# An adaLN block with sliding dilated attention and an MLP: softmax denominators from a ones column of V, K and Q weights loaded by halves, V of the first batch in four pieces, and another written-out order

## The chip, the cores and the metric

The kernel runs on one core of a Trainium2 chip. The core has a matrix engine (TensorE, PE in the profile, with its weight loads as PEld), a vector engine (VectorE, DVE), an activation engine (ScalarE, ACT), a general engine (GpSimd, POOL) and a queue engine (SyncE, SP), which here issues nearly all DMAs. The metric is the device time of one execution in microseconds (us); lower is better. All engines work through their own instructions in order and wait for each other by semaphores.

## The reference

S = 2048 rows, D = 448, H = 16 heads of 28, window of 8 keys at distance 2, F = 1792; all inputs are bf16.

```python
mod = silu(c) @ w_mod                      # six vectors of 448: sa, ca, ga, sb, cb, gb
h = layernorm(x) * (1 + ca) + sa
q, k, v = split_heads(h @ wqkv)
# key w of row s is row s - 2*w, for w = 0..7; rows before 0 are masked
attn = softmax(q . k / sqrt(28))           # over the 8 keys
x = x + ga * (attn @ v) @ wo
h = layernorm(x) * (1 + cb) + sb
x = x + gb * (gelu(layernorm(h) @ w1 + b1) @ w2 + b2)
```

## The kernel before

**Layout.** Even and odd rows never meet in the attention, so the sequence is two interleaved streams of 1024 rows (NS = 2), which lie side by side in every tile. The rows are cut into 8 tiles p of 128 (times 2 streams). D = 448 is three blocks of 128 and a rest of 64 rows; the rest's matmuls are those at L553, in 64-row tiles of the array. Heads stand 32 apart (HP) in the transposed tensors, 28 of them used.

**Front (tiles in units [0], [1], [2,3], [4,5], [6,7]).** Per tile: bn_stats and bn_aggr on DVE, the power -1/2 (`rstd`, on ACT or POOL), normalize on DVE into a buffer `zy` (five of them), a copied tail, a transpose. Units 0 and 1 are transposed by TensorE; the others by a DMA transpose on SP (`zT`). Then `affine` (L501/L503) applies the modulation and gives `hT`. K and Q of units 0 and 1 come from weights spread to a 32-wide head pitch (`spread`, `Wqk`, `Wqr`); those of tiles 2 to 7 are made in natural layout from the unspread staging tiles (`natural_qk`), evacuated into a `zy` buffer and transposed by DMA into `kT`, `qT` (L630).

**Attention in 9 batches of 114 queries.** `v{i}` makes V of the batch; `lt` the logits (two halves), ACT the exponentials (L744), DVE the mask (L750). `pd{i}` (L759) multiplies the weights `et` by a matrix of ones, which gives every one of the 32 output partitions of a head the denominator; `po{i}` (L770) multiplies them by V. ACT turns the denominators into reciprocals by Ln (L779, read from PSUM) and Exp (L781); DVE multiplies (`omul`, L787) into `qT`, over the queries. The V buffer's four spare columns of each head are zero. `out_proj` then makes wo, the residual, the second and third normalization and the transposed MLP input `yT`.

**MLP in 4 tiles of 256 rows (two p each):** `w1`, Gelu on ACT, `w2`, residual, store.

**Phases.** Batches 0 to 4, then MLP tile 0; batches 5 and 6, then MLP tile 1; batches 7 and 8, then MLP tiles 2 and 3. Each switch between Exp and Gelu loads an activation table (L924, L931).

**Order.** Nothing is scheduled at run time. Each `add(...)` makes a numbered task; `ORDER` lists the numbers, and this is the order in which they are issued, so each engine's own order is the list's order restricted to that engine. A suffix (`:A`, `:D`, `:P`, `:R`) takes another engine, or for `:R` another variant. `55+12@55` issues twelve filler matmuls of 256 columns on zeros (L381) ahead of task 55. `SLOTS` gives each tile its buffer; all PSUM tiles share four double banks (room "P").

Of the kernel before, what the change touches and what calls it, by code (L numbers as in the profile page):

```python
# [9 lines left out]
FP32 = mybir.dt.float32  # L10
# [5 lines left out]
KT, KS = 4, 64  # L16
# [50 lines left out]
455 369 434 371 490 372 456 403 443 491 488 435 444 404:D 457 405 458 459 493 492 436 494 460 437 495 461 594 517 438  # L67
462 496 497 463 536 498 499 595 525 500 537 596:D 524 538 539 466 464 501 502 467 465 518 503 528 468 526 527 470 505
529 504 506 531 469 519 507 530 521 471 520 510 472 523 540 522 543 475 508 553 532 541 476 473 533 474 509 542 511
535 562 565 534 477 551 557 512 513 552 563 514 478 515:D 566 479 564 600 480 597 567 554 544 598 481 601 568 445 569  # L70
570 602 547 555 571 599 556 548 572 516 603 604 605 545 606 573 628 607 546 574 608 635 609 549 610 550 636 611 439
575 630 640 576 612 629 637 577 639 613 578 614 638 579 641 581 633 580 634 582 632 583 631 586 647 584 585 587 616
588 615 648 617 642 656 645 618 644 621 649 589 658 622 619 646 620 643 623 650 664 625 590 624 591 651 626:D 592 654
662 653 627 665 655 657 652 663 659 674 660 666 667 669 661 675 668 676 678 677 679 686 672 673 670 687 681 671 690
680 691 688 689 694 693 701 683 692 682 684 695 685 702 697 703 704 709 698 696 710 699 705 711 700 706 712 707 708
# [77 lines left out]
def kernel(  # L153
# [74 lines left out]
    ones_k = cst.tile([128, 2, HP], BF16, name="ones_k")  # L228
# [16 lines left out]
    def dconst(us, fn, writes):  # L245
        early.append(add("DVE", us, fn, writes=writes, after=[one], name="const " + writes[0]))
# [44 lines left out]
    def consts():  # L291
        for vb in vbufs:
            nc.vector.memset(vb[:, :, :, DH:HP], 0.0)
        nc.vector.memset(ones_k[:], 1.0)
        nc.vector.memset(ones_k[0:WIN - 1, 1, :], 0.0)

    dconst(0.45, consts, ["vpad", "ones"])
# [25 lines left out]
    def load_qk(kt):  # L323
        load(lambda: nc.sync.dma_start(out=wqk_st.t[:, kt, :], in_=A_wqkv[kt * 128:kt * 128 + 128, 0:2 * D + HP - DH]), 0.62, [f"wqk{kt}"],
             bufs=[wqk_st])

    def load_rest(a):
        load(lambda a=a: nc.sync.dma_start(out=wqr_st.t[KS * a:KS * a + KS, :], in_=A_wqkv[(KT - 1) * 128:D, 0:2 * D + HP - DH]),
             0.5, [f"wr{a}"], bufs=[wqr_st])
# [20 lines left out]
    for kt in range(KT - 1):  # L350
        load_qk(kt)
    load_x(1, 2)
    load_rest(0)
    load_rest(1)
    load_x(2, 4)
    load_wv()
# [33 lines left out]
    add("PE", 0.45, c_cols, mode="32x128", reads=["c", "c1", "one1", "warm_w"], bufs=[psc], fills=[psc], name="c_cols")  # L390
    add("ACT", 0.12, lambda: nc.scalar.activation(out=e_c[:], in_=psc.t[:, 0, 0:128 * KT:128], func=ACT.Exp, scale=-1.0), bufs=[psc],
# [39 lines left out]
    def spread(half):  # L431
# [3 lines left out]
        for ks in [[k] for k in range(KT - 1)]:  # L435
            k0, n = ks[0], len(ks)
            dst, src = (lambda k0=k0, n=n: Wqk[:, k0:k0 + n, half]), (lambda k0=k0, n=n: heads(wqk_st.t[:, k0:k0 + n, half * D:half * D + D], H))
            add("DVE", 0.06 + 0.18 * n, lambda dst=dst, src=src: nc.vector.tensor_copy(out=dst(), in_=src()), reads=[f"wqk{k}" for k in ks],
                bufs=[wqk_st], writes=[f"W{half}{k}" for k in ks], port=True, name="spread",
                alt={"ACT": (0.13 + 0.43 * n, lambda dst=dst, src=src: nc.scalar.copy(out=dst(), in_=src())),  # L440
                     "POOL": (0.1 + 0.5 * n, lambda dst=dst, src=src: nc.gpsimd.tensor_copy(out=dst(), in_=src()))})

        for a in range(2):
            rows, c0 = slice(KS * a, KS * a + KS), half * D + a * D // 2
            src = lambda rows=rows, c0=c0: heads(wqr_st.t[rows, c0:c0 + D // 2], H // 2)
            add("DVE", 0.22, lambda rows=rows, src=src: nc.vector.tensor_copy(out=Wqr[rows, half], in_=src()), reads=[f"wr{a}"],
# [62 lines left out]
    def front_ln(u, on_act, dma=False):  # L509
# [5 lines left out]
        for q, p in enumerate(u):  # L515
# [3 lines left out]
            rstd(0, 2 * p, 2, on_act)  # L519
# [59 lines left out]
    def front_qk(u):  # L579
        last_qk.clear()  # L580
        n, c0 = 128 * len(u), LEAD + 128 * u[0]
        for half in range(2):
# [13 lines left out]
            for k in range(2):  # L596
                first = u[0] == k == 0
                last_qk.extend(summed([item(k, a) for a in range(2)], NS * n / 2400 + 0.0025,
                                      ([] if first else [f"W{half}{k}" for k in range(KT - 1)] + [f"h{kt}_{p}" for kt in range(KT - 1) for p in u] + rk), [pqs[k]], [pqs[k]], after=last_qk[-2:] if small and k else (),
# [13 lines left out]
    def natural_qk(p):  # L613
        c0 = LEAD + 128 * p
        for half in (1, 0):
# [6 lines left out]
            summed([item(s) for s in range(NS)], 0.1895, [f"wqk{k}" for k in range(KT - 1)] + ["wr0", "wr1"] + [f"h{kt}_{p}" for kt in range(KT)],  # L622
# [54 lines left out]
    def attention(i, tbl, prev_w1):  # L677
# [19 lines left out]
        else:  # L697
            def vmm(kts, first):

                for s in range(NS):  # L700
                    for kt in kts:
                        rest = kt == KT - 1
                        rows = slice(KS * s, KS * s + KS) if rest else slice(0, 128)
                        for j in range(2):
                            nc.tensor.matmul(pv.t[WK * j:WK * j + WK, s, 0:D], lhsT=hT[rows, NS * kt + s, kc + j * WQ:kc + j * WQ + WK],  # L705
                                             rhs=Wv[rows, kt, :], start=first and kt == kts[0], stop=not first and kt == kts[-1],
# [6 lines left out]
            def v_first():  # L713
# [3 lines left out]
            add("PE", 7 * 0.1895 + 0.1, None, reads=["pads", "wv", "wvr0", "wvr1"] + [f"h{kt}_{p}" for kt in range(KT) for p in ps_], bufs=[pv, vb],  # L717
                fills=[pv], instr=32, name=f"v{i}",
                alt={"PE": (7 * 0.1895 + 0.1, v_last, "128x64", "64x64"), "PE2": (7 * 0.1895 + 0.1, v_first, "64x64", "128x64")})
# [4 lines left out]
                                                            in_=pv.t[:, :, 0:D].rearrange("p s (h d) -> p s h d", h=H)))})  # L724
        et = sb("et", [128, 4, 4 * NS, WE], BF16, "et")
# [27 lines left out]
        pd, po = psum("pd"), psum("po")  # L753

        def dmm():
            for j in range(2):
                rows = slice(WK * j, WK * j + WK)
                for r in range(4):
                    nc.tensor.matmul(pd.t[HP * r:HP * r + HP, j, 0:2 * SBE], lhsT=ones_k[rows, int(i == j == 0), :],  # L759
                                     rhs=et.t[rows, r].rearrange("p m c -> p (m c)"),  # L760
                                     start=True, stop=True, tile_position=(WK * j, HP * r))
# [200 lines left out]
```

## Time and profile before

| | |
|---|---|
| three runs | 171.62, 169.03 and 171.14 us; median 171.14 |
| profiled execution | 170.37 us, of which 168.6 us are the span from first to last instruction |
| PE busy | 160.9 us, 95% of the span |
| DVE, ACT, POOL busy | 113.2, 101.3 and 42.0 us |

In the profile, a group of instructions has its source line, engine, operation, tiles, shapes and count; then its busy time in us and the mean of one in ns; then the idle time of its engine ahead of it and who ended it. A timeline row has its start, its length, engine and line, and in brackets the engine's idle time before it with the releaser. In the rows of windows stand the busy us of each engine (and instructions) in a stretch.

### The profile page before, as it was taken

Reading aid. Unit: us, or ns where it says so; the run is one execution under the profiler, and the core shown is the slowest. Engines: PE = TensorE matmul, PEld = TensorE weight load, DVE = VectorE, ACT = ScalarE, POOL = GpSimd, SP = SyncE. Lnnn points to the kernel's source line nnn. Section 1 sums busy time; section 2 is a strip of 40 time slices with the busy share of each in tenths; the row PEclk is TensorE's granted clock in tenths of the full one; section 3 lists DMA queues with packets and bytes.
Section 4 is the critical chain, followed back from the end, with each engine's and each line's share of the span. In section 5 each row is a group of like instructions: output and inputs, shape, how many; then the busy total and the mean of one; then the engine's idle time right before and its main releaser. Section 6 shows DMA issues by size and latency. Waiting matters only on the chain.

```text
span 168.6 us, 4965 instructions
## 1 busy us (share of the span) xinstructions
PE 160.9 (95%) x2126; PEld 84.0 (50%) x2126; DVE 113.2 (67%) x277; ACT 101.3 (60%) x139; POOL 42.0 (25%) x69
## 2 busy tenths in 40 slices
PE   7999969987999999999999999999999999999992
PEld 4778535444554544435565443555544455344562
DVE  7869898758899969897837869465596940400112
ACT  3378888949379946869557167986318440099000
POOL 3235251002030400319300033850003156008100
PEclk9999999999999999999999999999999999999999
DMA  5999989699999799300150000028020006110002
GB/s 158 323 336 291 167 253 172 129 158 255 188 227 287 211 160 201 100 0 0 25 106 2 4 0 2 4 49 188 4 95 14 0 4 120 46 67 0 0 27 82
DMA packets 35573, 18.78 MB, mean 111 GB/s; under 512 B 28507, under 2 KB 34592, under 8 KB 35552
## 3 DMA queue, kind: packets, MB, share of 16 engines
q1 hardware_dynamic: 35548, 18.47, 47.6%
q8 instruction: 16, 0.26, 0.6%
q14 instruction: 5, 0.04, 0.1%
q10 hardware_dynamic: 4, 0.00, 0.0%
HBM read 9.81 MB, written 1.84 MB: 69 GB/s over the span
## 4 chain that ended last, share of the span: by engine, by line
PE 77%; DMA 13%; DVE 4%; issue 2%; POOL 2%; SPq 1%; ACT 1%; POOLq 0%; DVEq 0%
PE p L882 26%; PE p L547 22%; PE pw L802 7%; DMA zT<-zy 7%; PE pq L547 5%; PE p L553 4%; DMA x_all<-in_A_x_dram 4%; PE pv L547 3%; PE po L770 3%; DMA wm_st<-in_w_mod_dram 3%; PE lt L737 2%; DVE hT L501 2%; PE pv L705 2%; PE pd L759 1%; DVE stt L455 1%
## 5 line engine op out<-in xcount | busy, mean ns | idle before, releaser
L863 ACT ACTIVATE hm<-p,b_col 128x512 bf16<-128x512 f32 x56 | 33.6, 695 | 30.6 <-PE p L553 26.1
L882 PE MATMUL p<-w_s,hm 128*128 128x448 bf16 (+1 forms) x238 | 44.5, 342 | 0.0
L547 PE MATMUL p<-yT,w_s 128*128 128x512 bf16 x168 | 38.1, 380 | 0.0
L468 POOL TENSOR_TENSOR rs_all<-mvs,neg_half 128x2 f32<-128x2 f32 x23 | 16.4, 719 | 75.1 <-DVE mvs L457 75.1
L882 PEld LDWEIGHTS <-hm 128*128 128x128 bf16 x238 | 22.6, 98 | 18.9 <-issue 0.6
L547 PEld LDWEIGHTS <-w_s 128*128 128x128 bf16 x168 | 15.8, 98 | 21.0 <-issue 3.2
L888 DVE TENSOR_TENSOR x_all<-p,x1p 128x896 bf16<-128x896 f32 (+2 forms) x10 | 8.8, 899 | 23.7 <-PE p L882 23.7
L744 ACT ACTIVATE et<-lt 128x928 bf16<-128x928 f32 x18 | 16.1, 940 | 6.7 <-PE lt L737 6.6
L455 DVE BATCH_NORM_STATS2 stt<-x_all 128x6 f32<-128x448 bf16 x32 | 18.6, 610 | 1.6 <-DMA x_all<-in_A_x_dram 1.4
L547 PE MATMUL pq<-wqk_st,hT 128*128 128x448 bf16 x72 | 15.0, 353 | 1.8 <-DVE hT L501 1.5
L840 POOL TENSOR_TENSOR x1p<-x_all,gbb_bc 128x448 f32<-128x448 bf16 x16 | 16.5, 1060 | 0.0
L787 DVE TENSOR_TENSOR qT<-po,den 128x912 bf16<-128x912 f32 x9 | 10.0, 1106 | 7.1 <-ACT den L781 6.7
L802 PE MATMUL pw<-wo_s,qT 128*128 128x448 bf16 x64 | 13.1, 353 | 0.0
L750 DVE TENSOR_TENSOR et<-et,mask 128x928 bf16<-128x928 bf16 x18 | 11.0, 640 | 2.2 <-ACT et L744 2.1
L627 ACT CAST zy<-pq 128x896 bf16<-128x896 f32 x11 | 9.7, 911 | 2.7 <-issue 2.0
L809 DVE TENSOR_TENSOR x_all<-pw,x_all 128x896 bf16<-128x896 f32 x8 | 8.7, 1088 | 3.9 <-PE pw L802 3.9
L779 ACT ACTIVATE den<-pd 128x928 f32<-128x928 f32 x9 | 8.5, 952 | 4.7 <-PE pd L759 4.7
L818 DVE TENSOR_TENSOR h<-h,mod_bc 128x896 bf16<-128x896 bf16 x16 | 10.4, 655 | 0.2
L547 PEld LDWEIGHTS <-hT 128*128 128x128 bf16 x72 | 6.5, 98 | 8.1 <-DVE hT L501 2.0
L455 DVE BATCH_NORM_STATS2 stt<-h 128x6 f32<-128x448 bf16 x16 | 9.5, 611 | 0.1
L781 ACT ACTIVATE den<-den,den_bias 128x928 f32<-128x928 f32 x9 | 9.4, 1068 | 0.2
L802 PEld LDWEIGHTS <-qT 128*128 128x128 bf16 x64 | 6.0, 98 | 6.0 <-issue 0.4
(114 smaller groups left out, 177.3 us busy)
## 6 DMA issues: line engine op xcount, KB each, us to landing
w_s<-in_B_w_dram SPq DMA_DIRECT2D x7, 224.0 KB, 3.3
out_dram<-x_all SPq DMA_DIRECT2D x7, 224.0 KB, 2.0
x_all<-in_A_x_dram SPq DMA_DIRECT2D x3, 448.0 KB, 6.5
wmod<-in_w_mod_dram SPq DMA_DIRECT2D x3, 448.0 KB
w_s<-in_B_w_dram SPq DMA_DIRECT2D x3, 448.0 KB, 4.8
wqk_st<-in_A_wqkv_dram SPq DMA_DIRECT2D x3, 225.0 KB, 4.3
wm_st<-in_w_mod_dram SPq DMA_DIRECT2D x1, 672.0 KB, 4.6
x_all<-in_A_x_dram SPq DMA_DIRECT2D x2, 224.0 KB
```

The source lines that it names most:

```text
L455: add("DVE", 0.53, lambda: nc.vector.bn_stats(out=stt[:, w, b, 0:6], in_=src()), reads=reads, bufs=bufs, after=early if w == b == 0 else ( ...
L468: ways = {"POOL": (0.55 + 0.17 * n, lambda: nc.gpsimd.tensor_tensor(out=r, in0=v, in1=neg_half[:, 0:n], op=ALU.pow))}
L547: nc.tensor.matmul(out(), lhsT=lhs(kt, slice(0, 128)), rhs=rhs(kt, slice(0, 128)), start=first and kt == 0, stop=not first and kt == KT - 2)
L627: add("ACT", 0.80, lambda to=to, src=src: nc.scalar.copy(out=to(), in_=src()), bufs=[pq, st], reads=["zpad"], writes=[(st, 0)], name="evac ...
L744: exps.append(add("ACT", 0.83, lambda half=half, lt=lt: nc.scalar.activation(out=et.t[:, 2 * half:2 * half + 2].rearrange("p r m c -> p r ...
L750: nc.vector.tensor_tensor(out=ev, in0=ev, in1=mask[:], op=ALU.mult)
L787: nc.vector.tensor_tensor(out=qT[:, :, LEAD + q00:LEAD + q00 + 2 * WQ], in0=po.t[:, :, 0:NS * 4 * WQ].rearrange("p j (m c) -> p m j c", c=WQ),
L802: nc.tensor.matmul(pw.t[:, s, 0:D], lhsT=qT[:, KT * s + ft, LEAD + 128 * p:LEAD + 128 * p + 128], rhs=wo_s[:, ft, :], start=(ft == 0), sto ...
L818: add("DVE", 0.55, lambda vec=vec, op=op: nc.vector.tensor_tensor(out=h2.t[:], in0=h2.t[:], in1=vec.unsqueeze(1).to_broadcast([128, NS, D] ...
L840: add("POOL", 1.0, lambda n=n: nc.gpsimd.tensor_tensor(out=x1p.t[:, n, :], in0=xn(p, n), in1=gbb2_bc[:], op=ALU.add), reads=[f"x{p}", "gbb ...
L863: gelus.append(add("ACT", 0.585, lambda f=f, a=a, p1=p1s[g]: nc.scalar.activation(out=hm.t[:, f].rearrange("p n c -> p (n c)"), in_=p1.t[: ...
L882: nc.tensor.matmul(p2.t[:, n, 0:c1 - c0], lhsT=hm.t[:, f, n, q * 128:(q + 1) * 128], rhs=w2_s[:, f, c0:c1], start=(f == parts[0][0]), stop ...
```

## The change

Five things differ.

1. **Denominators.** `pd` is gone: no matrix of ones, no PSUM tile, no matmuls. Column 28 of each head in the V buffers is set to one, so `po` gives the sum of the weights in partition 28 of each group of 32. A DVE `stream_shuffle` out of PSUM copies this partition to all 32 (`spread_den`, 128x912, fp32). Ln then reads SBUF, and Ln and Exp have 57 columns a head instead of 58. For the first batch the first seven rows of the ones column are set to zero and, behind its `po`, back to one (`ones`).
2. **Loads.** wqkv's K columns (half 1) and Q columns (half 0) are two loads of the three full blocks, and the rests four small ones, instead of three loads of one block each and two of the rests.
3. **V of the first batch** is four tasks, one for each block of D, instead of one. The matmuls are the same.
4. **rstd of tile 0** is two tasks of one column, and some dependencies of `qk1` are looser.
5. **ORDER and SLOTS** are other lists throughout. Eight placeholders (`fl`) take a PSUM slot and issue nothing.

```diff
-    ones_k = cst.tile([128, 2, HP], BF16, name="ones_k")
...
         for vb in vbufs:
-            nc.vector.memset(vb[:, :, :, DH:HP], 0.0)
-        nc.vector.memset(ones_k[:], 1.0)
-        nc.vector.memset(ones_k[0:WIN - 1, 1, :], 0.0)
+            nc.vector.memset(vb[:, :, :, DH:DH + 1], 1.0)
+            nc.vector.memset(vb[:, :, :, DH + 1:HP], 0.0)
...
+    def load_half(half):
+        c0, c1 = half * D, half * D + D + half * (HP - DH)
+        load(lambda: nc.sync.dma_start(out=wqk_st.t[:, :, c0:c1], in_=rows128(A_wqkv[0:(KT - 1) * 128, c0:c1])), 1.15, [f"wqk{half}"], bufs=[wqk_st])
+        for a in range(2):
+            load(lambda a=a: nc.sync.dma_start(out=wqr_st.t[KS * a:KS * a + KS, c0:c1], in_=A_wqkv[(KT - 1) * 128:D, c0:c1]),
+                 0.2, [f"wr{half}{a}"], bufs=[wqr_st])
...
-            rstd(0, 2 * p, 2, on_act)
+            for b, m in ((2 * p, 1), (2 * p + 1, 1)) if p == 0 else ((2 * p, 2),):
+                rstd(0, b, m, on_act)
...
+            if i == 0:
+                for kt in range(KT):
+                    add("PE", 0.380 if kt < KT - 1 else 0.194, lambda kt=kt: vmm([kt], kt == 0), ...
...
+        ones = lambda value: nc.vector.memset(vb.t[0:WIN - 1, :, :, DH:DH + 1], value)
+        if i == 0:
+            add("DVE", 0.06, lambda: ones(0.0), reads=["vpad"], bufs=[vb], fills=[vb], name="ones")
...
-        def dmm():
-            for j in range(2):
-                rows = slice(WK * j, WK * j + WK)
-                for r in range(4):
-                    nc.tensor.matmul(pd.t[HP * r:HP * r + HP, j, 0:2 * SBE], lhsT=ones_k[rows, int(i == j == 0), :],
-                                     rhs=et.t[rows, r].rearrange("p m c -> p (m c)"),
-                                     start=True, stop=True, tile_position=(WK * j, HP * r))
...
-        den = sb("den", [128, 2, 4 * NS, WE], FP32, "den")
-        flat = lambda: den.t[:].rearrange("p j m c -> p j (m c)")
-        add("ACT", 0.87, lambda: nc.scalar.activation(out=flat(), in_=pd.t[:, :, 0:2 * SBE], func=ACT.Ln, scale=DEN_SCALE),
-            bufs=[pd, den], fills=[den], after=[tbl], name="ln_den")
+        den = sb("den", [128, 2, 4 * NS, WQ], FP32, "den")
+        add("DVE", 1.0, lambda: nc.vector.stream_shuffle(out=den.t[:].rearrange("p j m c -> p j (m c)"), in_=po.t[:, :, 0:NS * 4 * WQ], mask=[DH] * HP),
+            bufs=[po, den], fills=[den], name="spread_den")
+        add("ACT", 0.87, lambda: nc.scalar.activation(out=den.t[:], in_=den.t[:], func=ACT.Ln, scale=DEN_SCALE),
+            bufs=[den], fills=[den], after=[tbl], name="ln_den")
```

The orders, in task names, at the places that matter. `qk2_1nf` is tile 2, half 1, full blocks, `r` the rest; `w2_p_n_k` is tile p, stream n, k = 0 with 8 matmuls and k = 1 with 6; `stats0_5` is normalization 0, tile 2, stream 1.

```
PE at the start
 before: 12 fillers, c_cols, 11 fillers, mod_cols ..., tr0, 9 fillers, qk0 ..., 3 fillers, ...
 after:  c_cols, 22 fillers, mod_cols ..., tr0, mod_cols ..., 10 fillers, qk0 ...
POOL: mask1, mask
 before: mask1 behind rstd0_4 and ahead of tail0_2, mask three tasks later
 after:  second and third task of POOL
SP loads
 before: x0 wm0 wmr0 wmr1 x1 wqk0 wr1 wr0 wqk1 wqk2 x2-3 x6-7 wv ...
 after:  x0 wm0 wmr0 wmr1 x1 wqk1 wqk0 x2-3 wr11 wr10 wr00 wr01 x6-7 x4-5 wv ...
DVE from the first stats of tile 3 to the affine of unit [2,3]
 before: 10 stats, 10 aggr, 4 norm, 1 tail, evac_h
 after:  12 stats, 12 aggr, 6 norm, 1 tail, evac_h
Phase 0, DVE from x1_0 to the last norm of yT1
 before: x1 2, stats 8, aggr 8, norm 8, h2 4, mask 4, omul3, windows6, b1_col; tail2_1 (DVE)
 after:  x1 2, stats 8, aggr 8, norm 8, h2 4, mask 4, omul3, spread_den3, spread_den4; tail2_1 (POOL)
Phase 0, DVE ahead of that, what changes engine
 before: evac_h 11 of 12 on DVE, windows5, 7, 6, 8 on DVE, evac_n3_0 on DVE
 after:  evac_h 7 of 12, windows5 alone; evac_n3_0 and evac_n3_1 on DVE; spread_den0, 1, 2; ones 2
Phase 0, PE end, after: po4 wo_2 v6f qk6_0nf v6r qk6_0nr b1 wo_3 w1_0
Phase 1, PE
 before: pd5 po5 po6 pd6 w2_0_1_0 w2_0_1_1 v8f wo_4 wo_5
 after:  po5 po6 v8r v8f w2_1_0_1 w2_1_1_1 w1_1_6 wo_4 wo_5
 DVE after: spread_den5 spread_den6 evac_v8 omul5 omul6
Phase 2, PE
 before: pd7 po7 w2_2_1_0 w2_2_1_1 pd8 po8 w2_2_0_0 wo_6 w2_2_0_1 wo_7
 after:  po7 w2_2_0_1 po8 w2_3_1_1 w2_3_0_0 w2_3_0_1 wo_6 wo_7
 DVE after: spread_den7 norm norm spread_den8 omul7 fin2 omul8
```

More of the change, by code (lines that the diff above doesn't have):

```diff
@@ L390 @@
     add("PE", 0.45, c_cols, mode="32x128", reads=["c", "c1", "one1", "warm_w"], bufs=[psc], fills=[psc], name="c_cols")
+    for i in range(8):
+        idle = psum("idle")
+        add("PE", 0.0, lambda: None, reads=["warm_w"], bufs=[idle], fills=[idle], instr=0, name=f"fl{i}")
     add("ACT", 0.12, lambda: nc.scalar.activation(out=e_c[:], in_=psc.t[:, 0, 0:128 * KT:128], func=ACT.Exp, scale=-1.0), bufs=[psc],
@@ L437, in spread @@
             dst, src = (lambda k0=k0, n=n: Wqk[:, k0:k0 + n, half]), (lambda k0=k0, n=n: heads(wqk_st.t[:, k0:k0 + n, half * D:half * D + D], H))
-            add("DVE", 0.06 + 0.18 * n, lambda dst=dst, src=src: nc.vector.tensor_copy(out=dst(), in_=src()), reads=[f"wqk{k}" for k in ks],
+            add("DVE", 0.06 + 0.18 * n, lambda dst=dst, src=src: nc.vector.tensor_copy(out=dst(), in_=src()), reads=["wqk1"] + ["wqk0"] * (1 - half),
                 bufs=[wqk_st], writes=[f"W{half}{k}" for k in ks], port=True, name="spread",
@@ L445, in spread @@
             src = lambda rows=rows, c0=c0: heads(wqr_st.t[rows, c0:c0 + D // 2], H // 2)
-            add("DVE", 0.22, lambda rows=rows, src=src: nc.vector.tensor_copy(out=Wqr[rows, half], in_=src()), reads=[f"wr{a}"],
+            add("DVE", 0.22, lambda rows=rows, src=src: nc.vector.tensor_copy(out=Wqr[rows, half], in_=src()), reads=[f"wr{half}{a}"] + ["wr11"] * (1 - half) * a,
                 bufs=[wqr_st], writes=[f"Wr{half}{a}"], port=True, name="spread r",
@@ L598, in front_qk @@
                 last_qk.extend(summed([item(k, a) for a in range(2)], NS * n / 2400 + 0.0025,
-                                      ([] if first else [f"W{half}{k}" for k in range(KT - 1)] + [f"h{kt}_{p}" for kt in range(KT - 1) for p in u] + rk), [pqs[k]], [pqs[k]], after=last_qk[-2:] if small and k else (),
+                                      ([] if first else [f"W{half}{k}" for k in range(KT - 1)] + [f"h{kt}_{p}" for kt in range(KT - 1) for p in u] + rk), [pqs[k]], [pqs[k]], after=last_qk[-1 if u[0] == 0 else -2:] if small and k else (),
                                       name=f"qk{u[0]}_{half}" + "ab"[k], split=rk if first else None))
@@ L705, in vmm @@
                             nc.tensor.matmul(pv.t[WK * j:WK * j + WK, s, 0:D], lhsT=hT[rows, NS * kt + s, kc + j * WQ:kc + j * WQ + WK],
-                                             rhs=Wv[rows, kt, :], start=first and kt == kts[0], stop=not first and kt == kts[-1],
+                                             rhs=Wv[rows, kt, :], start=first and kt == kts[0], stop=not first and kt == kts[-1] and (kt == KT - 1 or i > 0),
                                              tile_position=(rows.start, WK * j))
```

75 lines of the change are left out of this document (35 added, 40 removed), and 20 rows, old and new, of tables (ORDER, SLOTS).

## The prediction

> **What bounds the kernel now.** I read the page's shares first, then the windows of three stretches, then the timeline at each place where PE stood idle.
>
> ```profile
> PE 160.9 (95%) x2126; PEld 84.0 (50%) x2126; DVE 113.2 (67%) x277; ACT 101.3 (60%) x139; POOL 42.0 (25%) x69
> PE   7999969987999999999999999999999999999992
> DVE  7869898758899969897837869465596940400112
> ```
> ```profile
> 0.00:23.00 23.00, 20.05 (x312) 14.05 (x313) 18.87 (x79) 15.07 (x25) 8.81 (x27) 1.00 0.90 256
> 23.00:64.80 41.80, 40.03 (x771) 20.38 (x773) 35.45 (x79) 31.37 (x39) 5.72 (x8) 1.00 0.99 202
> 64.80:168.60 103.80, 100.84 (x1047) 49.53 (x1046) 58.88 (x121) 54.84 (x77) 27.44 (x35) 1.00 0.18 43
> 44.20:60.40 16.20, 16.20 (x360) 8.61 (x359) 15.81 (x38) 12.71 (x16) 3.15 (x4) 1.00 0.89 225
> ```
>
> PE works 95% of the span, but the three stretches are not alike. From 64.8 us on (the first MLP tile) PE has no gap until its last matmul, some 3 us before the end: whatever leaves PE's queue there shortens the run. Between 44.2 and 60.4 DVE is busy 15.81 of 16.20 us, so there are two full engines, and PE's share alone does not tell which one sets the time.
>
> ```profile
> 21.12 1.80 DVE L501 TENSOR_SCALAR hT<-zT,mod_col 128x512 bf16<-128x512 bf16 x3 [0.68 <-DMA zT<-zy]
> 22.97 2.44 PE L547 MATMUL pq<-wqk_st,hT 128*128 128x448 bf16 x12 [1.47 <-DVE hT L501]
> 39.13 0.39 PE L759 MATMUL pd<-et,ones_k 64*32 64x464 bf16 x8 [1.30 <-ACT zy L627]
> 44.21 1.09 DVE L809 TENSOR_TENSOR x_all<-pw,x_all 128x896 bf16<-128x896 f32 x1 [0.43 <-PE pw L802]
> 58.97 2.90 SPq L833 DMA_TRANSPOSE yT<-zy  x2
> 60.13 0.20 DVE L490 COPY zy<-zy 128x128 bf16<-128x128 bf16 x1
> 64.78 0.61 PE L553 MATMUL p<-yT,w_r 64*128 64x512 bf16 x4
> ```
> ```profile
> DMA to landing us min/median/max: 3.8/3.8/3.8
> ```
>
> PE waits 1.47 us for the affine of unit [2,3], which waits for the transposed DMA, and 1.30 us for a PSUM buffer. The second hidden limit is the last row: `tail2_1` on DVE ends at 60.33, its transpose is issued at about 60.5 (half of two issues in 2.90 us) and lands 3.8 later, at 64.3; the first MLP matmul starts at 64.8. The MLP therefore has only 0.5 us of room towards the DVE chain that feeds yT1.
>
> **The change part by part.** *Matmuls of the denominators.*
>
> ```profile
> 85.48 0.32 PE pd L759 x8
> 87.01 0.24 PE pd L759 x8
> 112.14 0.32 PE pd L759 x8
> 115.76 0.32 PE pd L759 x8
> ```
> ```profile
> L759 PE MATMUL pd<-et,ones_k 64*32 64x464 bf16 x72 | 3.5, 364 | 1.3 <-ACT zy L627 1.3
> ```
>
> In the chain of waits the four pd of phases 1 and 2 take 1.2 us, and nothing is idle there: **-1.2**. The five of phase 0, at 0.32 to 0.39, are 1.7 us; whether those count depends on what starts the MLP. `po` keeps its shape (a head's 32 columns of V, of which four were zeros), so the sum itself costs PE nothing.
>
> *Shuffles.* Nine DVE instructions of 128x912 out of PSUM are new; no row shows a shuffle.
>
> ```profile
> L723 DVE CAST vb<-pv 128x896 bf16<-128x896 f32 x1 | 1.0, 1049 | 0.0
> L628 DVE CAST zy<-pq 128x896 bf16<-128x896 f32 x1 | 1.1, 1080 | 0.0
> L311 DVE MEMSET wo_s<- 128x896 f32 x1 | 0.8, 805 | 0.1
> ```
>
> The nearest rows are the casts, which read PSUM one operand wide in the same size: 1.08 us is my value. The lower end is the fp32 write alone, 0.81; as upper end I take two passes, 2.16. [...]
>
> *Latency of a batch.*
>
> ```profile
> L779 ACT ACTIVATE den<-pd 128x928 f32<-128x928 f32 x9 | 8.5, 952 | 4.7 <-PE pd L759 4.7
> L781 ACT ACTIVATE den<-den,den_bias 128x928 f32<-128x928 f32 x9 | 9.4, 1068 | 0.2
> L787 DVE TENSOR_TENSOR qT<-po,den 128x912 bf16<-128x912 f32 x9 | 10.0, 1106 | 7.1 <-ACT den L781 6.7
> ```
> ```profile
> 112.46 0.55 PE po L770 x64
> 78.20 2.75 PE p L882 x14
> 91.15 3.03 PE pw L802 x16
> 94.17 1.29 PE p L547 x6
> ```
>
> From masks to `omul`: before, pd 0.32, Ln 0.95, Exp 1.07; after, po 0.55, shuffle 1.08, Ln, Exp: +1.3 us, and +0.1 if Ln out of SBUF takes Exp's time. Is it covered in phases 1 and 2? One w2 matmul is 2.75/14 = 0.196 us. Phase 1, from the end of po5: two shuffles end at 2.2, Ln5 at 2.0, Exp5 at 3.1, Ln6 at 4.1, Exp6 at 5.1, omul6 at 6.2. PE meanwhile has po6 0.55, v8 1.5 (8 matmuls as wide as wo's 16 in 3.03), 12 w2 2.4 and w1_1_6 1.5 (1.29 and the rests), so wo_4 at 5.9 (needs omul5, 4.4) and wo_5 at 7.4 (needs 6.2): 1.2 us of room. Phase 2, from the end of po7: PE has 6 w2, po8, 20 w2 = 5.7, wo_7 at 7.2; DVE and ACT (with two norms, a tail and fin2 between) end omul8 at 6.5: 0.7 us of room. So **0** in both, with the cover named; shuffles at 2.16 would bring about 1.0 and 1.5 us back as waits.
>
> *Start.* Its matmuls lose their early fillers.
>
> ```profile
> 1.25 2.74 PE L381 MATMUL ps_c<-warm_w 128*128 128x256 bf16 x12 [1.25 <-DVE warm_w L241]
> 3.93 0.60 PE L388 MATMUL ps_c<-one,c_row 1*128 1x128 bf16 x4
> 4.46 2.11 PE L381 MATMUL ps_col<-warm_w 128*128 128x256 bf16 x11
> 6.69 0.62 PE L409 MATMUL ps_col<-silu_bc,wm_st 128*128 128x32 bf16 x18
> 8.26 1.14 PE L381 MATMUL pq<-warm_w 128*128 128x256 bf16 x9
> ```
>
> The first 12 fillers take 0.22 us each (from 1.25 to 3.93), those at 8.26 0.13, the eleven between 0.19. The granted clock reads 1.00 throughout, so it does not show this. PE needs about 4.2 us of work (1.25 to some 5.5) to become fast. Afterwards c_cols comes first, at 3.9 at the latest, and 22 fillers follow: some 16 at 0.22 and 6 at 0.13 end at about 8.8, and mod_cols behind them moves from 6.7 to 8.6 or so; all at 0.13 it would be 7.4. [...]
>
> ```profile
> 12.39 1.68 DVE L455 BATCH_NORM_STATS2 stt<-x_all 128x6 f32<-128x448 bf16 x3 [1.44 <-DMA x_all<-in_A_x_dram]
> 6.33 0.95 SPq L338 DMA_DIRECT2D x_all<-in_A_x_dram  x2
> 17.21 0.29 POOL L489 COPY zy<-zy 128x128 bf16<-128x128 bf16 x1
> ```
>
> Does that count? DVE waited 1.44 us for tiles 2 and 3 anyway. Their load now has 225 KB less ahead of it, and would land near 11.5; but DVE, whose affine of tile 0 waits for mod_cols, gets there at about 12.3. POOL's mask no longer delays `tail0_2` (17.21), which helps; but ahead of the affine of unit [2,3] there now stand two stats, two aggr and two norms more. Before, 10 stats, 10 aggr, 4 norms and a tail took 12.39 to 20.44; the longer list, in the same measure, takes 10.2: affine from 22.5, ended at 23.6. PE's own queue comes at about 23. So qk2 starts at 23.6 instead of 22.97: **+0.7**, between -1.5 (the stall gone) and +1.5. Loading K and Q by halves, V in four pieces and the split rstd change no PE work, and I give them nothing of their own.
>
> *Phase 0.* What DVE is relieved of:
>
> ```profile
> L501 DVE TENSOR_SCALAR hT<-zT,mod_col x11: 405/411/1146, 21.1 to 39.2; 128x512 bf16<-128x512 bf16 x11
> L688 DVE COPY hw<-hT 128x1024 bf16<-128x1024 bf16 x4 | 1.7, 427 | 0.1
> ```
>
> An affine takes DVE 0.41 us, a copy of windows 0.43. From hT of unit [2,3] to x1_0 it took 44.21 - 22.97 = 21.2 us. Walking both queues with the durations above, I find no wait on pd2's PSUM buffer (1.30), wo_0 at 41.4 and x1_0 at 43.1, **-1.1**; DVE's extra shuffles 0 to 2 and evac_n3_1 are paid there by the four evac_h and windows7 that leave DVE. From x1_0 on, DVE is full. The old list took 44.21 to 60.33 = 16.1 us; the new has two shuffles more (2.16 by their records, 1.9 in the queue, where the rows overlap by some 14%) and lacks windows6, b1_col and the tail (0.7), so 17.3: last norm at 60.4, tail on POOL 0.3 to 0.5, transpose issued at 60.9, landing 64.7. PE's own queue could be there at about 63, for it lost 1.7 us of pd; it waits. The MLP starts at 64.8: **0**.
>
> Sum: 168.6 + 0 (the start's +0.7 is inside the 43.1) - 1.2 = 167.4 span; the profiled execution has 1.77 outside it (170.37), so 169.2, or 1.2 less than profiled. The median of the runs shown is 171.14, 0.8 above the profiled one; on that footing I forecast **169.9**.
>
> **The rivals.** (a) *PE sets the end everywhere.* If the DVE chain is ready earlier (x1_0 at 41.8 instead of 43.1, or a cheaper shuffle), all nine pd count, 2.9, and the stall at 39.13 too, 1.3: span 164.4, on the median's footing 166.9; with the stall at 22.97 gone as well, 165.5. For it: PE has 95%, and the idle DVE time before 44 us is 6.3 us (41.80 - 35.45) over the whole stretch. Against it: 15.81 of 16.20.
>
> (b) *Slower: DVE's queue becomes the bound of phase 0.* Ahead of yT1, DVE gets five shuffles (5.4), one evacuation (1.08) and two small memsets (0.14), and loses four affines at 0.41 (1.6), windows7 and 6 (0.9) and a tail (0.2): +3.9 net. If the idle time between 23 and 44 us sits where DVE waits for transposes and cannot take it, all of it reaches yT1, beyond the 0.5 us of room: 168.6 + 3.9 - 1.2 = 171.3, or 173.8 on the median's footing. It decides as soon as x1_0 comes later than about 43.5. With shuffles at 2.16, five times 1.08 more, it would be 179.
>
> (c) *The saving comes back in phases 1 and 2*: the latency of +1.4 exceeds the room of 1.2 and 0.7, by another DVE task in front of `omul`; then 1.2 returns as waits, span 168.6 to 169.5, 171.1 to 172 on that footing.
>
> **How the numbers follow.** My walk (168.5 to 171) 0.45; (a) 0.30; (b) 0.15; (c) 0.10. Low end 165.6, which leaves out the last of (a); high end 173.5, which leaves out most of (b) with the dearer shuffles. Some 2% is what a measurement of this kernel can tell from no change (the three runs differ by 1.5%): faster means under 167.7, most of (a), 0.28; slower means over 174.6, the far part of (b), 0.07; the rest 0.65.
>
> **What would show it.** Right: no pd rows; shuffles near 1.08; fillers at 0.22 until about 8 and mod_cols after 8; a wait of PE for yT or for wo_2, wo_3 ahead of the first MLP matmul, near 64.8; no PE idle behind it. Wrong: the MLP starts before 63 (rival a) or after 66.5 (rival b), or PE waits for omul at wo_5 or wo_7 (c), or a shuffle is far from 1.08.

## The result and the profile after

| | median us | runs | ratio to before, with 95% interval |
|---|---|---|---|
| before | 170.20 | 171.62, 169.03, 171.14, 169.26 | |
| after | 171.62 | 171.40, 171.83, 172.84, 171.38 | 1.0109 [1.0064, 1.0154] |

The change made the kernel 1.1% slower, by 1.4 us between the medians and 1.9 by the ratio; I had forecast a gain of 1.2. The profiled execution after took 171.4 us, its span 169.7 (before 170.37 and 168.6).

First the page of the kernel after: busy times, slices, and the chain that ended last.

```profile
PE 160.3 (94%) x2052; PEld 82.5 (49%) x2052; DVE 127.1 (75%) x290; ACT 104.8 (62%) x149; POOL 44.9 (26%) x72
PE   2999999899999899999999999999999998899993
DVE  5989979987999989899797976888977961300023
PE 50%; DVE 23%; DMA 8%; POOL 6%; ACT 5%; issue 4%; SPq 2%; ACTq 0%; POOLq 0%
```

PE has 0.6 us less to do than before, yet the run is longer, so PE now waits somewhere. The two 8s near the end of its row (slices 34 and 35, 140 to 148 us) say where. The timeline of the kernel after, at the places that the prediction named:

```profile
3.82 4.87 PE L377 MATMUL ps_col<-warm_w 128*128 128x256 bf16 x22
8.49 0.68 PE L409 MATMUL ps_col<-silu_bc,wm_st 128*128 128x32 bf16 x18
23.16 1.01 PE L548 MATMUL pq<-wqk_st,hT 128*128 128x448 bf16 x3
42.78 1.08 DVE L812 TENSOR_TENSOR x_all<-pw,x_all 128x896 bf16<-128x896 f32 x1
62.97 1.25 PEld L805 LDWEIGHTS <-qT 128*128 128x128 bf16 x8 [0.23 <-DVE qT L790]
64.50 1.67 PE L548 MATMUL p<-yT,w_s 128*128 128x512 bf16 x7
85.70 1.36 PE L771 MATMUL po<-et,vb 64*32 64x57 bf16 x128 [0.20 <-DVE et L759]
145.04 2.32 PE L548 MATMUL p<-yT,w_s 128*128 128x512 bf16 x10 [1.46 <-DMA yT<-zy]
```

In this execution nothing is lost up to the MLP's start (64.50; 64.78 before). The last row is the first up-projection of MLP tile 3, and it waits 1.46 us for a transposed tile. Before, PE came there at 143.84 and did not wait. What feeds that tile, in the timeline of the kernel after and then of the kernel before:

```profile
131.30 4.48 POOL L843 TENSOR_TENSOR x1p<-x_all,gbb_bc 128x448 f32<-128x448 bf16 x4
131.49 2.00 DVE L477 TENSOR_SCALAR h<-x_all,mvs,rs_all 128x448 bf16<-128x448 bf16 x2
133.53 2.73 DVE L821 TENSOR_TENSOR h<-h,mod_bc 128x896 bf16<-128x896 bf16 x2
137.97 0.70 POOL L468 TENSOR_TENSOR rs_all<-mvs,neg_half 128x2 f32<-128x2 f32 x1 [2.19 <-DVE mvs L457]
139.47 0.53 POOL L489 COPY zy<-zy 128x128 bf16<-128x128 bf16 x2 [0.80 <-DVE zy L477]
140.02 1.23 SPq L836 DMA_TRANSPOSE yT<-zy  x1
141.30 0.57 SPq L895 DMA_DIRECT2D out_dram<-x_all  x1
141.93 1.29 SPq L836 DMA_TRANSPOSE yT<-zy  x1
```
```profile
132.05 0.66 DVE L477 TENSOR_SCALAR h<-x_all,mvs,rs_all 128x448 bf16<-128x448 bf16 x2
132.75 1.28 DVE L818 TENSOR_TENSOR h<-h,mod_bc 128x896 bf16<-128x896 bf16 x2
135.90 0.69 POOL L468 TENSOR_TENSOR rs_all<-mvs,neg_half 128x2 f32<-128x2 f32 x1 [2.95 <-DVE mvs L457]
137.81 2.61 SPq L833 DMA_TRANSPOSE yT<-zy  x2
137.87 4.02 POOL L840 TENSOR_TENSOR x1p<-x_all,gbb_bc 128x448 f32<-128x448 bf16 x4
143.84 2.75 PE L547 MATMUL p<-yT,w_s 128*128 128x512 bf16 x12
```

Read each block from the `x1p` row. Before, GpSimd makes the four sums of residual and bias (`x1p`) after the tails, at 137.87, when the transposes are under way. After, it makes them at 131.30, and VectorE normalizes row tile 7 at the same time. Each of VectorE's four instructions there takes two to three times as long: 2.00 us for two norms (0.66 before), 2.73 for two h2 (1.28, the products of L821). GpSimd itself takes 4.48 instead of 4.02, but it has been idle for 2.19 us when the statistics for row tile 7's `rstd` arrive (137.97): VectorE was late, not GpSimd. Then the store of row tile 0 stands between the two transposes in SP's queue (0.57). So yT7 is issued at 141.93 and lands at 145.00.

The groups of the new instructions, with the group of h2:

```profile
L780 DVE STREAM_SHUFFLE den<-po 128x912 f32<-128x912 f32 x9 | 10.5, 1182 | 0.0
L782 ACT ACTIVATE den<-den 128x912 f32<-128x912 f32 x9 | 8.7, 962 | 7.5 <-DVE den L780 7.3
L821 DVE TENSOR_TENSOR h<-h,mod_bc 128x896 bf16<-128x896 bf16 x16 | 12.9, 807 | 0.2
```

A shuffle takes 1.18 us, and Ln costs the same from SBUF as from PSUM (0.96 and 0.95).

### The profile page after: what moved, and what is told of

The parts are those of the page before. It is cut to its first block, busy times and chain, and to the rows that moved or that the text cites. A ratio compares the mean times of both kernels' runs of the same rounds, so it can differ in the third digit from the quotient of the medians.

```text
span 169.7 us, 4856 instructions
## 1 busy us (share of the span) xinstructions
PE 160.3 (94%) x2052; PEld 82.5 (49%) x2052; DVE 127.1 (75%) x290; ACT 104.8 (62%) x149; POOL 44.9 (26%) x72
## 4 chain that ended last, share of the span: by engine, by line
PE 50%; DVE 23%; DMA 8%; POOL 6%; ACT 5%; issue 4%; SPq 2%; ACTq 0%; POOLq 0%
PE p L885 14%; PE p L548 11%; DVE stt L455 6%; PE pw L805 6%; PE pq L548 5%; DMA zT<-zy 3%; PE ps_col L377 3%; POOL rs_all L468 3%; DVE h L821 3%; DVE et L759 3%; POOL x1p L843 3%; PE po L771 2%; DVE w_s L661 2%; DVE zy L477 2%; PE pv L548 2%
## 5 line engine op out<-in xcount | busy, mean ns | idle before, releaser
L468 POOL TENSOR_TENSOR rs_all<-mvs,neg_half 128x2 f32<-128x2 f32 (+1 forms) x20 | 15.1, 757 | 56.4 <-DVE mvs L457 54.3
L843 POOL TENSOR_TENSOR x1p<-x_all,gbb_bc 128x448 f32<-128x448 bf16 x16 | 18.2, 1164 | 0.0
L782 ACT ACTIVATE den<-den 128x912 f32<-128x912 f32 x9 | 8.7, 962 | 7.5 <-DVE den L780 7.3
L821 DVE TENSOR_TENSOR h<-h,mod_bc 128x896 bf16<-128x896 bf16 x16 | 12.9, 807 | 0.2
L628 ACT CAST zy<-pq 128x896 bf16<-128x896 f32 x10 | 9.0, 904 | 3.6 <-DMA yT<-zy 1.6
L780 DVE STREAM_SHUFFLE den<-po 128x912 f32<-128x912 f32 x9 | 10.5, 1182 | 0.0
L784 ACT ACTIVATE den<-den,den_bias 128x912 f32<-128x912 f32 x9 | 9.5, 1057 | 0.2
L477 DVE TENSOR_SCALAR h<-x_all,mvs,rs_all 128x448 bf16<-128x448 bf16 x16 | 7.5, 494 | 2.5 <-POOL rs_all L468 2.4
```

The costliest lines, as they stand in the source:

```text
L468: ways = {"POOL": (0.55 + 0.17 * n, lambda: nc.gpsimd.tensor_tensor(out=r, in0=v, in1=neg_half[:, 0:n], op=ALU.pow))}
L477: add("DVE", 0.31, lambda: nc.vector.tensor_scalar(out=dst(), in0=src(), scalar1=mvs[:, w, b, 0:1], scalar2=rs_all[:, w, b:b + 1], op0=ALU ...
L780: add("DVE", 1.0, lambda: nc.vector.stream_shuffle(out=den.t[:].rearrange("p j m c -> p j (m c)"), in_=po.t[:, :, 0:NS * 4 * WQ], mask=[DH ...
L821: add("DVE", 0.55, lambda vec=vec, op=op: nc.vector.tensor_tensor(out=h2.t[:], in0=h2.t[:], in1=vec.unsqueeze(1).to_broadcast([128, NS, D] ...
L843: add("POOL", 1.0, lambda n=n: nc.gpsimd.tensor_tensor(out=x1p.t[:, n, :], in0=xn(p, n), in1=gbb2_bc[:], op=ALU.add), reads=[f"x{p}", "gbb ...
```

## The experiments

What makes small effects legible here is that the stretch behind the MLP's start repeats, while phase 0 does not. With the end of the last matmul taken as its group's start plus its length (before: 154.85 + 10.79 = 165.64; after: 157.55 + 9.28 = 166.83):

| kernel | ratio [95%] | MLP start | start to MLP tile 2 | start to end |
|---|---|---|---|---|
| before | 1 | 64.78 | 57.47 | 100.86 |
| after | 1.0109 [1.0064, 1.0154] | 64.50 | 57.32 | 102.33 |
| e13_after_again | 1.0114 [1.0064, 1.0164] | 65.89 | 57.32 | 102.38 |
| e1_gate_late | 1.0015 [0.9982, 1.0048] | 66.84 | 57.32 | 100.79 |
| e8_store_late | 1.0098 [1.0062, 1.0133] | 64.90 | 57.32 | 101.87 |
| e3_no_pd_late | 0.9970 [0.9933, 1.0006] | 66.04 | 56.87 | 100.26 |
| e7_more_visits | 1.0100 [1.0063, 1.0138] | 64.31 | 58.35 | 102.58 |
| e4_early_fill | 1.0055 [1.0023, 1.0087] | 65.04 | 56.97 | 101.99 |
| e6_fewer_visits | 1.0153 [1.0100, 1.0206] | 64.61 | 58.82 | 102.29 |
| e15_po5_later | 1.0115 [1.0074, 1.0155] | 65.52 | 58.09 | 101.56 |
| e5_ones_before | 1.0587 [1.0534, 1.0640] | 72.82 | 59.79 | 103.18 |
| e12_recolour_before | 1.0016 [0.9986, 1.0046] | 63.58 | 57.48 | 100.86 |
| e9_halves_before | 1.0107 [1.0067, 1.0147] | 67.10 | 57.48 | 100.86 |
| e14_v_pieces_before | 0.9990 [0.9959, 1.0022] | 64.65 | 57.48 | 100.86 |

Four kernels with before's order behind the MLP's start give 100.86, and two profiles of the kernel after 102.33 and 102.38, while the MLP's start of that same kernel moved by 1.4 us between two executions (64.50, 65.89). A difference of 0.1 us in the last column is therefore readable where the same waits occur, though the ratios alone resolve only 0.5 to 0.8 us. e4 is the exception: it has the order after in this stretch and is 0.34 shorter, because one wait (ahead of po5, below) did not occur in it. The profile of e1_gate_late fell in an execution with a longer phase 0, so only its last two columns are used.

**Is it the place of the sums?** (e1, e8; the kernel after with tasks moved)

```
e1  POOL: - gate2, x1p5_0, x1p4_0, x1p5_1, x1p4_1 between rstd2_12 and rstd2_14
          + the same five behind tail2_6
    SP:   - store0_00 between yT6 and yT7     + behind yT7
e8  SP:   the same move of store0_00 alone
```

> The changed kernel with one stretch of its order put back: in phase 3 the gate and the four x1p of MLP tile 2 stand on GpSimd behind rstd2_14 and both tails (as in the kernel before), and on SP the transpose yT7 stands ahead of the store. Theory W (the time was lost where PE waits for yT7: 1.46 us at 145.04): the norms and h2 beside x1p go back from 1.00 and 1.36 us to 0.39 and 0.64, yT7 lands before PE needs it, PE does not wait, and the time is 1.4 us less than the changed kernel's, 0.99 to 1.00 of the kernel before. Rival S (slots and switches of the array's tile size over the whole run are what costs): PE's wait goes, but the last matmul comes less than 0.5 us earlier, ratio 1.01.

The timeline of e1_gate_late, at the same instructions:

```profile
133.84 0.70 DVE L477 TENSOR_SCALAR h<-x_all,mvs,rs_all 128x448 bf16<-128x448 bf16 x2
134.57 1.28 DVE L821 TENSOR_TENSOR h<-h,mod_bc 128x896 bf16<-128x896 bf16 x2
145.75 2.75 PE L548 MATMUL p<-yT,w_s 128*128 128x512 bf16 x12
```

The norms are back to 0.70 for two, the h2 to 1.28, and the up-projection has no wait. The stretch is 1.54 us shorter (102.33 to 100.79), and the ratio 1.0015. Within this stretch, that is the whole loss.

> The kernel after with one move: the store of row tile 0 goes behind the last transposing DMA in SP's queue; the bias and residual sums of GpSimd stay where they were. If the queue of SP is what makes row tile 7 late, the wait of TensorE at 145 us goes: ratio 1.002. If it is mostly GpSimd (the sums ahead of the last rstd, and the VectorE operations slowed beside them), only the 0.6 us of the store go: TensorE still waits 0.8 us, ratio 1.006.

```profile
144.96 2.76 PE L548 MATMUL p<-yT,w_s 128*128 128x512 bf16 x12 [0.99 <-DMA yT<-zy]
```

In the timeline of e8_store_late 0.99 us of the wait are left, 0.47 are gone, and the stretch is 0.46 shorter (102.33 to 101.87). The ratio (1.0098) is too coarse to show this. So the store has a third of the wait, and VectorE, slowed beside GpSimd's sums, two thirds.

**What were the denominators' matmuls worth?** (e3: the kernel before, batches 5 to 8 without their `pd`; Ln's place is taken by an Exp on a column of `po`, so the denominators of these batches are not made.)

```diff
-        add("PE", 0.25, dmm, ...
+        add("PE", 0.25, dmm if i < 5 else lambda: None, ...
```

> The kernel before, but batches 5 to 8 make no denominators: their pd matmuls are left out and ACT reads one column of po as often as it read pd, so its time stays. Nothing else moves. This measures what the pd of phases 1 and 2 were worth to PE. My prediction's step: 1.2 us less from the first MLP matmul to the first of MLP tile 2 (57.57 us before), ratio 0.993. Rival S: each po then pays the switch of tile size that pd paid ahead of it (0.09 us), and its own record grows from 0.55 to 0.61, so 0.7 to 0.9 us less, ratio 0.995 to 0.996.

The stretch is 0.60 us shorter, not 1.2, and less than the 0.7 to 0.9 of rival S. Ends of matmuls are modelled, so I go from the start of a group to the start of the next. Timelines of the kernel before, then of e3, at batches 5 and 6 and at batch 8:

```profile
85.41 0.39 PE L759 MATMUL pd<-et,ones_k 64*32 64x464 bf16 x8
87.19 2.82 PE L882 MATMUL p<-w_s,hm 128*128 128x448 bf16 x14
115.69 0.39 PE L759 MATMUL pd<-et,ones_k 64*32 64x464 bf16 x8
116.56 1.69 PE L882 MATMUL p<-w_s,hm 128*128 128x448 bf16 x8
```
```profile
86.84 1.32 PE L770 MATMUL po<-et,vb 64*32 64x57 bf16 x128
88.10 2.82 PE L882 MATMUL p<-w_s,hm 128*128 128x448 bf16 x14
116.62 0.68 PE L770 MATMUL po<-et,vb 64*32 64x57 bf16 x64
117.23 1.69 PE L882 MATMUL p<-w_s,hm 128*128 128x448 bf16 x8
```

Batches 5 and 6 hold PE for 1.26 us instead of 1.78, batch 8 for 0.61 instead of 0.87: 0.52 and 0.26 less, where the rows of `pd` in the chain said 0.56 and 0.32. The difference I put down to a fee: the first group in another tile size of the array pays for the change of size (in the chain a `pd` that opens a visit shows 0.32 us, the one behind `po6` 0.24; e7 below prices a change), `pd` had paid it for `po`, and I had read it as the matmuls' own time. Batch 7 should gain 0.26 too, 1.04 in all, but the down-projection behind its `po` comes 0.14 late (for what, I did not find). Two more waits appear in e3: po5 comes 0.16 late, behind VectorE (the 20 matmuls ahead of it take 4.05 us to its start instead of 3.89), and wo_5 0.14 late, its weight load behind `omul` (wo_4 and wo_5 take 3.17 instead of 3.03). So 1.04 us left PE's queue, and 0.44 came back as waits.

**What does a change of tile size cost?** (e7: the kernel before, the same matmuls, 14 changes of tile size more)

```
- w1_2_2f w1_2_2r w1_2_0r w1_2_0f w1_2_4f w1_2_6f w1_2_6r w1_2_4r
+ w1_2_2f w1_2_2r w1_2_0f w1_2_0r w1_2_4f w1_2_4r w1_2_6f w1_2_6r      (so in all four MLP tiles)
```

> The kernel before, only the order of the up-projection's pieces changed: each remainder (64 rows) directly behind its own main piece, so that TensorE changes its tile size 14 times more, with the same matmuls. By theory S (about 0.09 to 0.12 us for each change) 1.3 to 1.7 us longer behind the MLP's start: ratio 1.0075 to 1.010. By the rival (a change of tile size costs nothing, and the pitch in the records is only how ends are modelled) 0 us: ratio 0.998 to 1.002.

The timelines of MLP tile 2, first before, then e7_more_visits (`64*128` are the rests):

```profile
122.25 2.75 PE L547 MATMUL p<-yT,w_s 128*128 128x512 bf16 x12
124.94 1.04 PE L553 MATMUL p<-yT,w_r 64*128 64x512 bf16 x8
125.91 6.65 PE L547 MATMUL p<-yT,w_s 128*128 128x512 bf16 x30
132.49 0.82 PE L553 MATMUL p<-yT,w_r 64*128 64x512 bf16 x6
```
```profile
122.66 2.75 PE L547 MATMUL p<-yT,w_s 128*128 128x512 bf16 x12
125.34 0.61 PE L553 MATMUL p<-yT,w_r 64*128 64x512 bf16 x4
125.88 2.76 PE L547 MATMUL p<-yT,w_s 128*128 128x512 bf16 x12
128.58 0.61 PE L553 MATMUL p<-yT,w_r 64*128 64x512 bf16 x4
```

From start to start, a visit of eight rests takes 0.97 us (124.94 to 125.91) and a visit of four 0.54 (125.34 to 125.88), so two of four cost 0.11 more, without the change ahead of the second. Over the stretch it is 102.58 - 100.86 = 1.72 us. Inside the stretch there are 46 changes instead of 31, for the order before makes one of its own just ahead of the start; 1.72 us for 15 changes is 0.115 us each. The ratio agrees (1.010).

With this price the account from the MLP's start to its tile 2 can be drawn up, where the kernel after gains only 0.15 us (57.47 to 57.32). All terms are from start to start:

- The visits with `po` shrink from 1.78 to 1.29 us (batches 5 and 6) and twice from 0.87 to 0.61 (batches 7 and 8): -1.01.
- The order after has 26 changes of tile size, the order before 23: one more visit of logits and one more of the rests, and two visits that stand directly beside another. At e7's price, 0.115 us, taken for every size: +0.35.
- po5 waits for its mask (the row at 85.70). The 22 matmuls ahead of it take 4.54 us to its start; in e4, where po5 does not wait, 4.27: +0.27.
- wo_6 (118.78) starts 0.34 us after the matmul ahead of it instead of 0.19, its weight load behind a residual on VectorE; wo_4 and wo_5 take 0.06 more than before (3.09 and 3.03): +0.21.

The rows of the third point, the kernel after and then e4_early_fill:

```profile
81.16 4.33 PE L885 MATMUL p<-w_s,hm 128*128 128x448 bf16 x22
```
```profile
81.69 4.34 PE L885 MATMUL p<-w_s,hm 128*128 128x448 bf16 x22
85.96 1.25 PE L771 MATMUL po<-et,vb 64*32 64x57 bf16 x128
```

The sum is -0.18, against -0.15 measured. The saving was real, and the phases that earned it gave it back, in changes of tile size and in short waits.

**Does the start count?** (e4: the kernel after)

```
- PE: c_cols, 22 fillers, mod_cols
+ PE: 12 fillers, c_cols, 11 fillers, mod_cols
```

> The changed kernel with the fillers placed as before: 12 ahead of c_cols and 11 behind, instead of 22 behind. My prediction's step on the start: PE is fast by about 5.5 us again, mod_cols starts at about 6.7 to 7.2 instead of 8.49, and qk2 starts at about 22.5 instead of 23.16, limited by the transposed DMA; the MLP start at 64.50 is set by the DVE chain and moves by 0.3 us at most: ratio to the kernel before 1.008 to 1.011. Rival C (the cold start is carried through): everything up to the first MLP matmul comes 0.6 us or more earlier, and the time is 0.6 to 1.5 us less than the changed kernel's.

mod_cols came at 7.13 instead of 8.49, but the first product of unit [2,3] at 23.02 instead of 23.16, and the MLP's start was no earlier (65.04). The lower ratio (1.0055 against 1.0109) overlaps that of the kernel after; 0.34 us of it are the shorter stretch behind the MLP's start. So a start 1.36 us earlier moves the next stage by 0.14.

**Each part of the change alone, in the order before.** (All four are the kernel before.)

```
e5   denominators:  - pd5 po5 ... ln_den5     + po5 (where pd5 stood) spread_den5 ln_den5     (all nine batches)
e9   loads:         - wqk0 wr1 wr0 wqk1 wqk2  + wqk1 wr11 wr10 wqk0 wr01 wr00
     V, batch 0:    - lt1_1 lt1_0 v0          + v0k0 v0k1 lt1_1 lt1_0 v0k2 v0k3
e14  V, batch 0:    as in e9, nothing else
e12  SLOTS alone, dealt anew by the rule used for e5
```

> The kernel before with the denominators alone changed: ones column of V, shuffle, Ln from SBUF; po stands where pd stood and the shuffle directly ahead of Ln, PSUM slots given anew, the rest of the order and all loads as before. Theory D (the denominators cost DVE more than they give PE): nine shuffles at 1.18 us go into a DVE queue that is full between 44 and 60 us, the first MLP matmul moves from 64.8 to 66 or later, and PE waits for omul in phases 1 and 2; ratio 1.005 to 1.015. Theory O (the denominators are a gain and the new order lost it): ratio 0.99 to 0.995. A ratio of 1.00 within its interval would say that the two cancel.

> The kernel before with the two other parts of the change alone: K's and Q's columns of the weights loaded apart (K first, in the places of the old loads), and V of the first batch in four pieces, two of them ahead of the scores of batch 1. The denominators and the rest of the order stay. By my theory (the start is not on the path, and phase 0 is bound behind it) the ratio is 0.998 to 1.003 and the MLP starts at 64.5 to 66 us. By the rival (the weights' arrival sets the first product and all behind it) the first Q and K product moves by up to 1 us and the MLP's start with it: ratio 0.994 or 1.006.

> The kernel before with V of the first batch in four pieces alone, placed as in e9_halves_before; the weights load as before. In the trace of e9_halves_before the first product of Q and K already came 1.9 us late, behind casts that began at 9.99 where they began at 7.46 before, ahead of any V product. If that is the whole cost, this one is at 0.998 to 1.003. If the pieces cost too, it is at 1.005 or more.

> The kernel before with its PSUM slots dealt out anew by the same greedy rule as in e5_ones_before and e6_fewer_visits, and nothing else. If the 10 us of e5_ones_before and the waits of e6_fewer_visits are of the denominators and of the order, this is the kernel before: ratio 0.998 to 1.003. If they are of the slots (a product that waits for a slot's last reader), a good part of them is seen here: ratio over 1.01, with waits of TensorE for VectorE's omul.

e5 lost 10 us, far more than theory D said. e12 is as fast as the kernel before, so the rule by which slots are dealt anew is not the cause by itself. Most of the 10 us (8.0) lie ahead of the MLP's start, the rest behind it; the timeline of e5_ones_before shows the wait that my rival (b) and the latency step were about, at the output projections:

```profile
71.20 1.69 PE L796 MATMUL pw<-wo_s,qT 128*128 128x448 bf16 x8 [1.38 <-DVE qT L781]
99.62 1.69 PE L796 MATMUL pw<-wo_s,qT 128*128 128x448 bf16 x8 [0.93 <-DVE qT L781]
```

V in pieces costs nothing (e14). So the halves cost e9 its 1.8 us (by the ratio), all ahead of the MLP's start (64.78 to 67.10). The first cast of weights in the timeline of the kernel before, then e9_halves_before's ACT and PE:

```profile
7.46 0.62 ACT L440 COPY Wqk<-wqk_st 128x512 bf16<-128x512 bf16 x1 [1.00 <-DMA wqk_st<-in_A_wqkv_dram]
```
```profile
9.99 0.62 ACT L437 COPY Wqk<-wqk_st 128x512 bf16<-128x512 bf16 x1 [3.55 <-DMA wqk_st<-in_A_wqkv_dram]
11.13 0.38 PE L558 MATMUL pq<-hT,Wqk 128*128 128x256 bf16 x2 [1.47 <-ACT hT L500]
```

The cast begins at 9.99 instead of 7.46, when it needed the first third of the rows only, and the affine behind it in ACT's queue holds PE. In the kernel after, the same cast begins at 8.62, and the MLP starts no later than before (64.50): the new order makes up for what its parts cost in the old one.

**Better versions?** (e6 and e15: the kernel after with e1's moves and those below; e13: the kernel after, again)

```
e6   SLOTS dealt anew as in e12
     - w2_1_1_0 po5 po6 v8r v8f w2_1_0_1 w2_1_1_1 w1_1_6r     + w2_1_1_0 w2_1_0_1 po5 po6 w2_1_1_1 v8f v8r w1_1_6r
     - po7 w2_2_0_1 po8                                       + w2_2_0_1 po7 po8
e15  - w2_1_1_0 po5 po6 v8r v8f w2_1_0_1                      + w2_1_1_0 w2_1_0_1 po5 po6 v8r v8f
```

> The kernel after with the two moves of e1_gate_late, and three switches of the array's tile size less in phases 1 and 2: the value products of batches 7 and 8 side by side, those of batches 5 and 6 one down-projection piece later (so that they no longer wait for a mask, 0.20 to 0.27 us), and the V product of batch 8 beside the remainder of the up-projection. By theory S (a switch of tile size holds TensorE for about 0.1 us, and these visits ate what the denominators' matmuls had cost) the stretch from the MLP's start to its tile 2 shrinks from 57.5 to 57.0 us and the ratio goes from 1.0015 of e1_gate_late to 0.998 to 0.999. By the rival (the switches lie under other work) the stretch stays at 57.5 and the ratio at 1.001 to 1.002. If the cover of batches 7 and 8 is gone, TensorE waits for the output projection of row tile 6 or 7, up to 1 us, and the ratio is 1.004.

> The kernel after with the moves of e1_gate_late, and one piece of the down-projection of row tile 1 ahead of the value products of batch 5, which waited 0.20 to 0.27 us for a mask. If these 0.2 us were on the path, the MLP's start to its tile 2 goes from 57.46 to 57.25 us and the ratio from 1.0015 to 1.000. If not, or if the shorter cover of batches 5 and 6 shows (the output projection of row tile 4 waits), it is 1.0015 or more.

> The kernel after, unchanged, beside the others of this set, so that they can be compared with it on one chip. From the first comparison: ratio 1.006 to 1.015, and 1.46 us of wait ahead of the first up-projection product of MLP tile 3.

e13 repeats the result. e6 and e15 both came out slower than e1_gate_late. A row each of the timelines of e6_fewer_visits and e15_po5_later:

```profile
91.97 0.39 PE L553 MATMUL p<-yT,w_r 64*128 64x512 bf16 x2 [1.38 <-DVE qT L789]
```
```profile
95.80 1.67 PE L805 MATMUL pw<-wo_s,qT 128*128 128x448 bf16 x8 [0.86 <-DVE x_all L891]
```

In both the wait ahead of po5 is gone, and one behind it is longer. In e6 the up-projection waits for `omul`, which frees a PSUM buffer (and wo_6 and wo_7 wait another 0.48 together); as its slots were dealt anew, whether the order or the slots make this wait is not shown. In e15 wo_5 waits for the residual of row tile 1, which stands behind omul6 in VectorE's queue, and omul6 waits 0.83 us for its reciprocals, as it does in the kernel after; with po5 later, that chain ends later. The 0.2 us could not be had by one move. No version beat the kernel before: e1_gate_late equals it, and e3_no_pd_late does not make its result.

## Why the prediction was wrong

- **"No PE idle behind the MLP's start"** failed, and this step decided the sign. I compared the two orders in phases 0 to 2 and never read phase 3, where the change of denominators touches nothing but the order is another. A wait of 1.46 us stood there (1.54 by e1).
- **Matmuls of the denominators, -1.2**: nearly right as PE's work, wrong as time. The visits got 1.01 us shorter; most of the rest of the 1.2 is the fee of entering a tile size (0.32 us against 0.24 in the chain's rows), which `po` pays when `pd` is gone. But the sum had no term for three more changes of tile size (0.35) and put the waits in these phases at nothing (0.48 in the kernel after). 0.15 were left at MLP tile 2, and 0.07 at the end once the late tile of phase 3 was mended (e1).
- **Shuffles**: 1.18 us against 1.08, far from either bound.
- **Latency covered in phases 1 and 2**: held for `omul`; in the kernel after no output projection of these phases is seen to wait for it, only wo_6 for a residual (0.15). The order before does not cover it: in e5 wo_4 waits 0.93 us for `omul` (99.62).
- **Start and phase 0**: right in numbers, in part by luck. mod_cols came at 8.49 (8.6), but the 22 fillers began at 3.82 and all took 0.21 us; I had them begin later and six of them run at 0.13. The 4.2 us of work until PE is fast were an estimate that no run shows: before, the fillers go from 0.21 to 0.11 us from start to start at about 6.0, 4.7 us behind the first of them, and in the kernel after 22 of them in 4.87 us all stay at 0.21. The product of unit [2,3] came at 23.16 (23.6), x1_0 at 42.78 (43.1), the MLP at 64.50 (64.8). But I had PE wait there for yT1, and it does not: the up-projection follows wo_3 without a gap, and wo_3's weight load waited 0.23 us for the last `omul` of phase 0 (62.97). e4 shows that the start has slack.
- **Halves and V's pieces, "nothing of their own"**: right for V (e14). For the halves right only in the new order; in the old one they cost 1.8 us (e9).
- **Rivals**: (a) and (b) are out by the MLP's start. (c) gave the time that came, 171.1 to 172, by a return of the saving as waits; but the large one was for a transposed tile in phase 3, not for `omul`, and the 0.48 us in phases 1 and 2 were for a mask and a residual. That the figure agrees is luck.

Left open: the ratio of the kernel after (1.1%, 1.1 to 2.6 us) leaves room for some tenths in phase 0 beside the 1.5 us shown. Phase 0 moves by more than that from one execution to the next (the MLP of the kernel after started at 64.50 and 65.89), so these runs cannot tell.

## What to carry to other kernels

When an order is rewritten as a whole, compare it in every stage where the bounding engine has no slack, for each queue that feeds it, and not only where the arithmetic changes. When matmuls are removed, count the changes of the array's tile size before and after, and look for the waits that the shorter queue uncovers: here 1.0 us was removed and 0.15 remained. And find a stretch that repeats to 0.1 us between executions, read small effects there from start to start, and check that the same waits occur.

## What the runs showed of the hardware

- Beside GpSimd's fp32 sums, VectorE's norm rose from 0.35 to 1.00 us and its bf16 product from 0.64 to 1.36, while GpSimd slowed only from 4.02 to 4.48 for four. The two hindered each other, and were still quicker side by side than one after the other: the stretch from 131.30 to 136.26 is 4.96 us, and the two sequences alone take 4.02 (the kernel before) + 1.98 (e1_gate_late) = 6.00.
- A change of the array's tile size, between 128*128 and 64*128, cost TensorE 0.115 us (e7: 1.72 us for 15).
- A shuffle of 128x912 fp32 from PSUM to SBUF took 1.18 us, and the load of its mask 0.01.
